# First tile of a pooled-attention and feed-forward kernel: batch 1's k and v pooled by vector engines instead of by matmuls, attention sums split from values, and the down matmuls over four accumulators

## The chip, the cores and the metric

The kernel runs on one core of one Trainium2 chip. A core has a matrix engine (TensorE, PE in the profile; its weight loads are shown apart as PEld), three engines for elementwise work (VectorE or DVE, ScalarE or ACT, GpSimd or POOL), a queue engine (SyncE, SP), and 16 DMA engines that move data between HBM and the on-chip memory. TensorE writes to PSUM, which has eight banks of 512 float32 per partition. Each engine works through its own instructions in order and waits for others by semaphores.

The metric is the time of one execution on the device, in microseconds (us).

## The reference

There are 8 batches of 8 heads with 576 rows of 64 elements, in q, k and v. The values that feed the second half are computed so:

```python
pool = 8                                  # Sp = 576 / 8 = 72 pooled rows
k_p = k.reshape(B, H, Sp, pool, D).mean(axis=3)
v_p = v.reshape(B, H, Sp, pool, D).mean(axis=3)
scores = scale * np.matmul(q, k_p.transpose(0, 1, 3, 2))
attn = softmax(scores)
x = np.matmul(attn, v_p)                  # then [4608 tokens, 512]
h = x @ w_in                              # 512 x 2048
g = h * np.cos(h)
out = g @ w_out                           # 2048 x 512, float32
```

The kernel computes in bfloat16 with float32 sums. It leaves the maximum out of the softmax, and it takes 1/sum as exp(-ln(sum)).

## The kernel before

**Tiles.** The 4608 tokens are worked in nine tiles of 512. A tile has an *up half* (`up_mm`, line 321): eight groups `fp` of 2 x 4 matmuls of 128x128 by 128x512, each group into one of three PSUM pairs `banks[0..2]` (two banks each); ScalarE takes the cosine (line 328), VectorE multiplies into `g_sb` (line 331). Then a *down half* (`down_mm`, line 334): 64 matmuls `(ms, fc)`, 16 for each of four blocks of 128 tokens, accumulated in the two single banks `obanks`; `down_out` copies a finished block out (line 340) and SP stores it (line 344).

**Attention.** Batch b's attention is worked while tile b-1 is (tile 0 for batch 1), by calls that are put between the down matmuls; batch 0's is worked at the start. One *unit* is 256 tokens of four heads; the batch has four units and a last segment `REST` of 64 tokens of all heads, which is done in the next tile. A unit goes: `scores` (four matmuls, line 214, into a PSUM pair, then Exp on ScalarE, line 221), then `values`: four matmuls (line 244) whose weights hold the pooled v of a head beside 64 columns of 8.0 (`vz`), so that the same matmul gives the weighted values and the softmax sum on different partitions; then Ln and Exp on ScalarE (lines 250, 251) and a multiply on VectorE (line 255) into `xT`, the up matmuls' input.

At the start, batch 0 uses a second form: `sums_first` (line 269), matmuls with weights of ones that give the sums alone, and `values_then` (line 283), matmuls with 64-wide weights that give the values alone, four each for a unit.

**Pooling.** There are two ways in the kernel. Batches 0 and 1 are pooled by TensorE: k and v are loaded in a layout of 128 partitions (`load_even`, `kv_even_tiles`), and matmuls with a 0/1 matrix `groups` add eight rows (`pool_k_mm`, line 160, 72 matmuls for a batch, whose results are copied into `kk` by line 132; `pool_v_mm`, line 168, 18 matmuls, copied into `vz` by line 170). From batch 2 on, k and v are loaded with the 72 pooled rows on partitions and eight rows behind each other (`load_kv`), and GpSimd adds halves three times (`pool_add`, lines 142, 145, 148 and 151); k's result `kp2` is then transposed by a DMA (`k_transpose`). Batch 0 and 1's q is transposed by TensorE in 18 matmuls with an identity (`q_transpose_mm`, line 195).

**Order.** The schedule is written by hand: each engine runs its instructions in the order of the code. In the down half of a tile, `fill` is a list of pairs (number of the down matmul before which it is put, call). In tile 0, the down matmuls go over two blocks `ms` at a time and, inside, over the four slices of `w_out`:

```python
mms = [(ms, fc) for hm in range(2) for cg in range(4) for ms in range(2 * hm, 2 * hm + 2)
       for fc in range(4 * cg, 4 * cg + 4)]
```

**Loads.** All loads but one are issued by POOL in the order of the code: q, k, v of batch 0; three of four slices of `w_in`; k of batch 1; half of its q; the last slice of `w_in`; the other half of q; `w_out` 0; v of batch 1; `w_out` 1 to 3; then, in tile 0, k, q and v of batch 2, whose adds stand behind them in POOL's order. `kv_st` has two buffers: batch 1's k and v lie in one, and batch 2's k and v take the two in turn.

The constants `dist` and `sign` are used at the start to make `groups`, and not later.

Of the kernel before, what the change touches and what calls it, by code (L numbers as in the profile page):

```python
# [9 lines left out]
FP32 = mybir.dt.float32  # L10
# [9 lines left out]
def kernel(  # L20
# [62 lines left out]
    def load_even(dst, b, src, j0=0, j1=KCH):  # L83
        nc.gpsimd.dma_start(out=dst[:, j0:j1].rearrange("p j t d -> p j (t d)"), in_=even_view(src, b, j0, j1))

    def kv_tile():
        return kvst.tile([128, 2 * H * POOL * D], BF16, name="kv_st", tag="kv_st")
# [9 lines left out]
    def q_tile(b):  # L97
        staged["q", b] = qst.tile([128, KCH, ROW, D], BF16, name="q_b", tag="q_b")

    def load_kv(b, which, src):  # L100

        st = kv_tile()[:Sp].rearrange("p (i h t d) -> p i h t d", i=2, h=H, t=POOL)
        nc.gpsimd.dma_start(out=st[:, 0].rearrange("p h t d -> p h (t d)"),
                            in_=src[b].rearrange("h (p t) d -> p h (t d)", t=POOL))
        staged[which, b] = st

    def load_q(b):
        q_tile(b)
# [2 lines left out]
    def load_w_in(cg):  # L111
        nc.gpsimd.dma_start(
            out=w_in_sb[cg],
            in_=moe_w_in[:, cg * 512:(cg + 1) * 512].rearrange("(k p) f -> p k f", p=128))

    def load_w_out(cg):
        nc.gpsimd.dma_start(
            out=w_out_sb[cg],
            in_=moe_w_out[cg * 512:(cg + 1) * 512, :].rearrange("(f p) m -> p f m", p=128))
# [5 lines left out]
    def v_part(b):  # L125
        return vz[b % 2][:, :, 0:4:3, :]
# [4 lines left out]
            for r in range(2):  # L131
                copy(out=dst[half[r], pj0:pj1, a, 0:Sp], in_=ps[half[a]])

    def pool_add(b, which, part=None):

        st = staged[which, b]
        x = st[:, 0]
        s = st[:, 1].rearrange("p h t d -> p (h t d)").bitcast(FP32).rearrange(
            "p (h t d) -> p h t d", h=H, t=POOL // 2)
        add = nc.gpsimd.tensor_tensor  # L140
        if part != 1:
            add(out=s, in0=x[:, :, 0:4, :], in1=x[:, :, 4:8, :], op=ADD)  # L142
        if part == 0:
            return
        add(out=s[:, :, 0:2, :], in0=s[:, :, 0:2, :], in1=s[:, :, 2:4, :], op=ADD)  # L145
        if which == "k":
            for slot in range(2):
                add(out=kp2[b % 2][:Sp, :, slot, :], in0=s[:, :, 0, :], in1=s[:, :, 1, :], op=ADD)  # L148
        else:
            s = s.rearrange("p (j a) t d -> p j a t d", a=2)  # L150
            add(out=v_part(b), in0=s[..., 0, :], in1=s[..., 1, :], op=ADD)

    def pool_k_mm(b, bank, pj0, pj1):

        kb = staged["k", b]
        ps = bank[:, 0:(pj1 - pj0) * Sp].rearrange("p (j n) -> p j n", n=Sp)
        for pj in range(pj0, pj1):
            for t in range(ROW):
                for rows in half:
                    nc.tensor.matmul(ps[rows, pj - pj0, :], lhsT=kb[rows, pj, t, :], rhs=groups[rows, t, :],  # L160
                                     start=(t == 0), stop=(t == ROW - 1))
        return lambda copy: put_kk(b, ps, pj0, pj1, copy)
# [10 lines left out]
    def k_transpose(b):  # L173
        nc.sync.dma_start_transpose(out=kk[b % 2], in_=kp2[b % 2].rearrange("p h s d -> p (h s d)"))


    QB = KCH * ROW // 2

# [84 lines left out]
    def sums_first(b, u, cs):  # L263

        (c0, n), (h0, nh) = u
        ex = att["ex", b, u]
        for i in range(nh):
            hp = i % 2
            nc.tensor.matmul(cs[hp * 64:hp * 64 + 64, (i // 2) * n:(i // 2 + 1) * n], lhsT=ones[:Sp, :],
                             rhs=ex[:, ex_col(u, i):ex_col(u, i) + n])  # L270
# [4 lines left out]
        att["inv", b, u] = inv  # L275

    def values_then(b, u, ao):

# [103 lines left out]
    dist = consts.tile([128, ROW, Sp], FP32, name="dist")  # L382
    sign = consts.tile([128, ROW, Sp], FP32, name="sign")
# [10 lines left out]
    half_pi = consts.tile([128, 1], FP32, name="half_pi")  # L394
    nc.vector.memset(half_pi, math.pi / 2.0)

    kv_even_tiles(1)
    q_tile(1)
    for cg in range(3):
        load_w_in(cg)  # L400
    load_even(staged["k", 1], 1, k)
    load_even(staged["q", 1], 1, q, 0, 2)
    load_w_in(3)
    load_even(staged["q", 1], 1, q, 2, 4)
    load_w_out(0)
    load_even(staged["v", 1], 1, v)
    nc.gpsimd.memset(vz[1], float(POOL))
    for i in range(2):
        nc.gpsimd.memset(kp2[i], 0.0)
    for cg in range(1, 4):  # L410
        load_w_out(cg)

    def warm_up(n, bank):

# [41 lines left out]
    for t in range(NT):  # L456
        b = t + 1
        if t > 0:

            up_mm(t, 0, 0, 2)  # L460
            up_mm(t, 1, 0, 2)
        for fp in range(FFCH // 2):
            up_mm(t, fp, 2 if fp < 2 else 0)
            between = ()
            if t == 0:
                if fp == 4:
                    puts = pool_k_mm(1, obanks[0], 0, 2), pool_k_mm(1, obanks[1], 2, 4)
                elif fp in (5, 6):
                    g0 = 9 * (fp - 5)
                    puts = q_transpose_mm(1, obanks[0], g0, g0 + 5), q_transpose_mm(1, obanks[1], g0 + 5, g0 + 9)  # L470
                if fp in (4, 5, 6):
                    puts[0](vec)
                    between = ((puts[1], act),)
            up_g(t, fp, between)
            if 0 < t and b < B:
                if fp == 0:
                    q_transpose(b)
                elif fp == 2:
                    k_transpose(b)
                    if t == 1:  # L480
                        load_next(b)
                        pool_add(b, "v", 1)
                        load_kv(b + 1, "v", v)
        mms = [(ms, fc) for ms in range(4) for fc in range(FFCH)]
        if t == 0:
            mms = [(ms, fc) for hm in range(2) for cg in range(4) for ms in range(2 * hm, 2 * hm + 2)
                   for fc in range(4 * cg, 4 * cg + 4)]


        def S_(n, bank):  # L490
            return lambda: scores(b, us[n], banks[bank])

        later = []

        def V_(n, bank, wait=None):
            return lambda: values(b, us[n], banks[bank], wait)

        fill = []
        if t < B:
            exp_tables()  # L500
            fill = [(1, lambda: scores(t, REST, banks[2])), (16, lambda: values(t, REST, banks[1]))]
        if t == 0:
            fill[1:] = [(2, S_(0, 0)), (8, lambda: pool_v_mm(1, banks[1])), (8, lambda: values(t, REST, banks[2])),
                        (11, S_(1, 0)), (13, V_(0, 1)), (18, S_(2, 2)), (21, V_(1, 0, later)), (26, S_(3, 1)),
                        (32, lambda: later.pop()()), (32, V_(2, 2)), (40, V_(3, 0))]
        elif b < B:
            us = BY_TOKENS

            def scores_of(*parts):

                def go():
                    for f in scores_mm, scores_exp:
                        for b_, u, bank in parts:
                            f(b_, u, banks[bank])
                return go

            def rows_of(i, blk, bank):
                return lambda: values_rows(b, us[2 * i:2 * i + 2], blk, banks[bank])

            fill = [(4, scores_of((b, us[0], 2), (b, us[1], 0))), (18, rows_of(0, 0, 1)), (19, rows_of(0, 1, 2)),  # L520
                    (29, scores_of((b, us[2], 0), (b, us[3], 1), (t, REST, 2))),
                    (42, rows_of(1, 0, 0)), (44, rows_of(1, 1, 1)), (47, lambda: values(t, REST, banks[2]))]
        fi = 0
        if t == NT - 1:
            mms = mms[:-FFCH]
        for n, (ms, fc) in enumerate(mms):
            while fi < len(fill) and fill[fi][0] <= n:
                fill[fi][1]()
                fi += 1
            down_mm(obanks[ms % 2], ms, fc)  # L530
            if fc == FFCH - 1:
                down_out(t, ms, obanks[ms % 2])
        if t < B:
            sin_tables()
        if b + 1 < B:
            if t != 1:
                load_next(b)
                load_kv(b + 1, "v", v)
            pool_add(b + 1, "k")
            pool_add(b + 1, "v", 0 if t == 0 else None)  # L540
# [29 lines left out]
```

## Time and profile before

| what | value |
|---|---|
| time, median of 3 runs | 296.92 us (296.73 to 298.92) |
| the profiled execution: its time and its span | 296.36 us, 294.6 us |
| mean granted TensorE clock | 0.998 of full |
| PE, DVE, ACT, POOL busy | 98%, 54%, 55%, 44% of the span |
| DMA queue that POOL issues to | 18.07 MB, 39.4% of the 16 engines' time |
| up matmuls (line 321) | 576, 126.6 us busy |
| down matmuls (line 334) | 560, 131.4 us busy |
| score matmuls (line 214) | 192, 11.9 us busy |
| GpSimd's first pooling add (line 142) | 12, mean 4058 ns |
| tile 0's up half | 17.21 to 33.59 us |
| tile 0's down half | 33.59 to 52.96 us |
| tile 1 | 52.96 to 83.32 us |

A row of a timeline has the start, the length, the engine, the line in the code, the operation, output <- input, the shape and the count; in square brackets stands the idle time of the engine before it and what ended that. The chain of work that ended last is followed back from the last instruction: at each step to what released it. All times are microseconds from the start of the span. Matmuls are pipelined, so the time of one in a chain is the distance to the next, and its own row is longer.

### The profile page before, as it was taken

To read this page: it belongs to the slowest core of one execution; us is meant where nothing else is said; L and a number is where in the kernel's file an instruction comes from. 1 tells how busy PE (TensorE), PEld (TensorE's weight loads), DVE (VectorE), ACT (ScalarE), POOL (GpSimd) and SP (SyncE) were. 2 spreads that over 40 slices of the span, in tenths; PEclk is the share of its full clock that TensorE was granted. 3 is DMA by queue.
4 is the path that set the end of the run, shared out by engine and by line. 5 is a ranking of instruction groups with operands and counts; after the bars stand their busy time and mean duration, and the time that the engine had idled before them with its cause. 6 is when DMAs were issued, how large, how long until landed. Compare 5 with 4: busy or idle time off the path is not lost.

```text
span 294.6 us, 4775 instructions
## 1 busy us (share of the span) xinstructions
PE 287.7 (98%) x1912; PEld 140.2 (48%) x1912; DVE 158.8 (54%) x212; ACT 162.1 (55%) x182; POOL 130.5 (44%) x93
## 2 busy tenths in 40 slices
PE   8899999999999999999999999999999999999995
PEld 3545544444544454445444544455445544444444
DVE  5458647466347643764375456645574557416612
ACT  3886898365446734673468337743675456506500
POOL 8563017968973696349833983399000000000000
PEclk9999999999999999999999999999999999999999
DMA  7999999659966975698469747994603320131033
GB/s 151 204 207 206 207 205 207 137 95 178 157 155 93 167 128 131 112 170 149 108 122 169 147 92 139 162 148 103 142 2 71 81 64 0 36 73 36 0 71 73
DMA packets 57222, 36.07 MB, mean 122 GB/s; under 512 B 35185, under 2 KB 52465, under 8 KB 57201
## 3 DMA queue, kind: packets, MB, share of 16 engines
q0 software_dynamic: 19744, 18.07, 39.4%
q1 hardware_dynamic: 37216, 17.57, 28.6%
q8 instruction: 15, 0.25, 0.4%
q10 hardware_dynamic: 240, 0.13, 0.2%
q14 instruction: 7, 0.05, 0.0%
HBM read 36.70 MB, written 9.44 MB: 157 GB/s over the span
## 4 chain that ended last, share of the span: by engine, by line
PE 93%; DVE 1%; issue 0%; DVEq 0%
PE bank L321 42%; PE obank L334 42%; PE bank L214 3%; PE bank L301 2%; PE bank L244 1%; PE bank L352 1%; PE obank L160 0%; PE bank L168 0%; PE obank L283 0%; PE obank L195 0%; DVE xT L285 0%; DVE vz L170 0%; DVE o_sb L340 0%; DVEq L285 0%
## 5 line engine op out<-in xcount | busy, mean ns | idle before, releaser
L334 PE MATMUL obank<-w_out_sb,g_sb 128*128 128x512 bf16 x560 | 131.4, 379 | 0.0
L321 PE MATMUL bank<-xT,w_in_sb 128*128 128x512 bf16 x576 | 126.6, 379 | 0.0
L328 ACT ACTIVATE cos<-bank,half_pi 128x1024 f32<-128x1024 f32 x72 | 79.3, 1114 | 70.4 <-PE bank L321 70.4
L331 DVE TENSOR_TENSOR g_sb<-bank,cos 128x1024 bf16<-128x1024 f32 x72 | 87.3, 1223 | 51.6 <-ACT cos L328 51.6
L321 PEld LDWEIGHTS <-w_in_sb 128*128 128x128 bf16 x576 | 56.1, 98 | 67.6 <-issue 1.6
L334 PEld LDWEIGHTS <-g_sb 128*128 128x128 bf16 x560 | 51.6, 98 | 56.6 <-issue 2.0
L142 POOL TENSOR_TENSOR kv_st<-kv_st 72x2048 f32<-72x2048 bf16 x12 | 48.7, 4058 | 30.4 <-DMA kv_st<-in_k_dram 30.4
L340 DVE COPY o_sb<-obank 128x512 f32<-128x512 f32 x35 | 24.2, 692 | 46.9 <-PE obank L334 46.7
L221 ACT ACTIVATE ex<-bank 72x1024 bf16<-72x1024 f32 (+1 forms) x40 | 35.0, 929 | 21.2 <-PE bank L214 21.1
L145 POOL TENSOR_TENSOR kv_st<-kv_st 72x1024 f32<-72x1024 f32 x12 | 28.2, 2348 | 0.9
L250 ACT ACTIVATE lnc<-bank 64x256 f32<-64x256 f32 (+1 forms) x24 | 10.8, 449 | 17.9 <-PE bank L244 17.7
L255 DVE TENSOR_TENSOR xT<-bank,inv 64x256 bf16<-64x256 f32 (+1 forms) x24 | 12.3, 511 | 10.8 <-ACT inv L251 10.6
L304 DVE TENSOR_TENSOR x_r<-bank,inv_r 128x512 bf16<-128x512 f32 x24 | 16.6, 691 | 0.8
L148 POOL TENSOR_TENSOR kp<-kv_st 72x512 bf16<-72x512 f32 x12 | 14.9, 1265 | 0.5
L214 PE MATMUL bank<-qT,kk 64*72 64x256 bf16 (+1 forms) x192 | 11.9, 250 | 0.4 <-DVE qT L196 0.4
L214 PEld LDWEIGHTS <-kk 64*72 64x72 bf16 x192 | 7.9, 110 | 8.7 <-issue 7.4
L309 ACT ACT_TABLE_LOAD x9 | 11.5, 1283 | 0.9 <-PEq L554 0.7
L312 ACT ACT_TABLE_LOAD x9 | 11.5, 1283 | 0.2
L301 PEld LDWEIGHTS <-ex 72*128 72x128 bf16 x192 | 8.9, 97 | 5.0
L452 POOL COPY gate<-kk 1x1 bf16<-1x1 bf16 x5 | 0.9, 180 | 22.7 <-DMA kk<-kp 22.7
L302 DVE RECIPROCAL inv_r<-bank 128x8 f32<-128x8 f32 x24 | 4.8, 202 | 10.7 <-PE bank L301 10.7
L301 PE MATMUL bank<-vz,ex 72*128 72x65 bf16 x192 | 9.8, 192 | 0.0
(59 smaller groups left out, 113.9 us busy)
## 6 DMA issues: line engine op xcount, KB each, us to landing
out_dram<-o_sb SPq DMA_DIRECT2D x70, 128.0 KB, 2.4
kv_st<-in_v_dram POOLq DMA_DIRECT2D x8, 576.0 KB, 12.9
kv_st<-in_k_dram POOLq DMA_DIRECT2D x7, 576.0 KB, 7.9
q_b<-in_q_dram POOLq DMA_DIRECT2D x6, 576.0 KB, 10.0
w_in_sb<-in_moe_w_in_dram POOLq DMA_DIRECT2D x4, 512.0 KB, 13.4
w_out_sb<-in_moe_w_out_dram POOLq DMA_DIRECT2D x4, 512.0 KB, 18.2
q_b<-in_q_dram POOLq DMA_DIRECT2D x4, 288.0 KB, 12.2
g_sb<-in_k_dram SPq DMA_DIRECT2D x1, 576.0 KB, 3.6
```

Of the source, the lines that this page charges most:

```text
L142: add(out=s, in0=x[:, :, 0:4, :], in1=x[:, :, 4:8, :], op=ADD)
L145: add(out=s[:, :, 0:2, :], in0=s[:, :, 0:2, :], in1=s[:, :, 2:4, :], op=ADD)
L148: add(out=kp2[b % 2][:Sp, :, slot, :], in0=s[:, :, 0, :], in1=s[:, :, 1, :], op=ADD)
L214: nc.tensor.matmul(pair[:Sp, bank, c:c + n].rearrange("p (g n) -> p g n", n=64), lhsT=kk[b % 2][half[r], h0 + i, 0:Sp], rhs=att["qT", b][h ...
L221: nc.scalar.activation(out=ex[:, 0:nh * n].rearrange("p (a n) -> p a n", a=2), in_=pair[:Sp, :, 0:nh * n // 2], func=ACTF.Exp, scale=scale ...
L301: nc.tensor.matmul(out[:, pj, hp * (D + 1):(hp + 1) * (D + 1)], lhsT=ex[:, c:c + 128], rhs=v1)
L304: nc.vector.tensor_mul(out=x, in0=vals, in1=inv.unsqueeze(3).to_broadcast([128, KCH, 2, D]))
L321: nc.tensor.matmul(h[:, j, :], lhsT=w_in_sb[fc // 4][:, ki, (fc % 4) * 128:(fc % 4 + 1) * 128], rhs=xT[:, ki, t * TILE:(t + 1) * TILE], st ...
L328: nc.scalar.activation(out=cos, in_=h, func=ACTF.Sin, bias=half_pi[:, :1])
L331: nc.vector.tensor_mul(out=g_sb[:, 2 * fp:2 * fp + 2, :], in0=h, in1=cos)
L334: nc.tensor.matmul(o, lhsT=g_sb[:, fc, ms * 128:(ms + 1) * 128], rhs=w_out_sb[fc // 4][:, fc % 4, :], start=(fc == 0), stop=(fc == FFCH - 1))
L340: nc.vector.tensor_copy(out=o[:, 0:n], in_=ps)
```

## The change

It has five parts, all around tile 0.

1. Batch 1's k and v are loaded as those of later batches are, with 72 pooled rows on partitions, each in two halves of four heads, and are pooled by `pool_add`: k by GpSimd, v by VectorE, in halves of four heads. k's result is transposed by TensorE (`k_transpose_mm`, new: four matmuls with an identity for four heads, one copy), and not by a DMA. The 72 + 18 pooling matmuls of batch 1 are gone.
2. The order of POOL's loads and instructions before tile 0 is other: see the diff. Two of the buffers for constants, `dist` and `sign`, now lie in the memory of `w_out` 2 and 3.
3. In tile 0 the scores of batch 1 go two units at a time, and `sums_two` and `values_two` (new) take the place of `values`: first the sums of two units by matmuls with ones, with one Ln and one Exp for both; later the values of the two with one multiply.
4. The second half of q's transposes moves from the up half (group 6) to down matmul 14; the first half moves from group 5 to 6. The last segment of batch 0 moves from down matmuls 1 (scores) and 8 (values) to 44 and 52.
5. Tile 0's down matmuls go over the slices of `w_out` outermost, with all four blocks open in four accumulators: the two banks of `banks[2]` and the two `obanks`. The four blocks end with matmuls 51, 55, 59 and 63; the first is copied out with the second.

```diff
-    def load_kv(b, which, src):
+    def load_kv(b, which, src, h0=0, h1=H):
...
+        if (which, b) not in staged:
+            staged[which, b] = kv_tile()[:Sp].rearrange("p (i h t d) -> p i h t d", i=2, h=H, t=POOL)
+        nc.gpsimd.dma_start(out=staged[which, b][:, 0, h0:h1].rearrange("p h t d -> p h (t d)"),
+                            in_=src[b, h0:h1].rearrange("h (p t) d -> p h (t d)", t=POOL))
...
-    def pool_add(b, which, part=None):
+    def pool_add(b, which, part=None, add=nc.gpsimd.tensor_tensor, h0=0, h1=H):
...
+    def k_transpose_mm(b, bank, h0, h1):
+
+        ps = bank.bitcast(BF16)[:, 0:(h1 - h0) * Sp].rearrange("p (h n) -> p h n", n=Sp)
+        for h in range(h0, h1):
+            nc.tensor.matmul(ps[:, h - h0, :], kp2[b % 2][:Sp, h].rearrange("p s d -> p (s d)"), identity[:Sp, :Sp],
+                             is_transpose=True)
+        nc.vector.tensor_copy(out=kk[b % 2][:, h0:h1, 0:Sp], in_=ps)
...
+    def sums_two(b, us_, pair):
+
+        for u, cs in zip(us_, (pair[:, 0, :], pair[:, 1, :])):
+            (c0, n), (h0, nh) = u
+            for i in range(nh):
+                hp = i % 2
+                nc.tensor.matmul(cs[hp * 64:hp * 64 + 64, (i // 2) * n:(i // 2 + 1) * n], lhsT=ones[:Sp, :],
+                                 rhs=att["ex", b, u][:, ex_col(u, i):ex_col(u, i) + n])
+        inv = asb.tile([128, 2, 512], FP32, name="inv2", tag="inv2", bufs=2)
+        nc.scalar.activation(out=inv, in_=pair, func=ACTF.Ln)
+        nc.scalar.activation(out=inv, in_=inv, func=ACTF.Exp, scale=-1.0)
+        att["inv", b, us_] = inv
+
+    def values_two(b, us_, pair):
+
+        for i, u in enumerate(us_):
+            (c0, n), (h0, nh) = u
+            ex = att.pop(("ex", b, u))
+            for k in range(nh):
+                pj, hp = divmod(h0 + k, 2)
+                nc.tensor.matmul(pair[hp * 64:hp * 64 + 64, i, (k // 2) * n:(k // 2 + 1) * n],
+                                 lhsT=vz[b % 2][:, pj, 3 * hp, :], rhs=ex[:, ex_col(u, k):ex_col(u, k) + n])
...
+        nc.vector.tensor_mul(out=x, in0=pair.rearrange(both, n=n),
+                             in1=att.pop(("inv", b, us_)).rearrange(both, n=n))
...
-    kv_even_tiles(1)
     q_tile(1)
     for cg in range(3):
         load_w_in(cg)
-    load_even(staged["k", 1], 1, k)
+    load_kv(1, "k", k, 0, 4)
+    load_w_in(3)
     load_even(staged["q", 1], 1, q, 0, 2)
-    load_w_in(3)
+    load_w_out(0)
+    load_kv(1, "k", k, 4, 8)
     load_even(staged["q", 1], 1, q, 2, 4)
-    load_w_out(0)
-    load_even(staged["v", 1], 1, v)
-    nc.gpsimd.memset(vz[1], float(POOL))
     for i in range(2):
         nc.gpsimd.memset(kp2[i], 0.0)
-    for cg in range(1, 4):
-        load_w_out(cg)
+    nc.gpsimd.memset(vz[1], float(POOL))
+    load_w_out(1)
+    load_kv(1, "v", v, 0, 4)
+    pool_add(1, "k", h0=0, h1=4)
+    load_w_out(2)
+    load_kv(1, "v", v, 4, 8)
+    load_w_out(3)
+    pool_add(1, "k", h0=4, h1=8)
...
             if t == 0:
-                if fp == 4:
-                    puts = pool_k_mm(1, obanks[0], 0, 2), pool_k_mm(1, obanks[1], 2, 4)
-                elif fp in (5, 6):
-                    g0 = 9 * (fp - 5)
-                    puts = q_transpose_mm(1, obanks[0], g0, g0 + 5), q_transpose_mm(1, obanks[1], g0 + 5, g0 + 9)
-                if fp in (4, 5, 6):
+                if fp == 6:
+                    puts = q_transpose_mm(1, obanks[0], 0, 5), q_transpose_mm(1, obanks[1], 5, 9)
                     puts[0](vec)
                     between = ((puts[1], act),)
+                elif fp == 7:
+                    k_transpose_mm(1, obanks[0], 0, 4)
...
         if t == 0:
-            mms = [(ms, fc) for hm in range(2) for cg in range(4) for ms in range(2 * hm, 2 * hm + 2)
-                   for fc in range(4 * cg, 4 * cg + 4)]
+            mms = [(ms, fc) for cg in range(4) for ms in range(4) for fc in range(4 * cg, 4 * cg + 4)]
...
+        def late_q():
+            puts = q_transpose_mm(1, banks[0][:, 0, :], 9, 14), q_transpose_mm(1, banks[0][:, 1, :], 14, 18)
+            for put in puts:
+                put(vec)
+
+        def pool_v(h0):
+            return lambda: pool_add(1, "v", add=nc.vector.tensor_tensor, h0=h0, h1=h0 + 4)
+
+        early, late = tuple(us[0:2]), tuple(us[2:4])
+
+        def sums_values():
+            sums_two(1, late, banks[0])
+            values_two(1, early, banks[1])
...
         if t == 0:
-            fill[1:] = [(2, S_(0, 0)), (8, lambda: pool_v_mm(1, banks[1])), (8, lambda: values(t, REST, banks[2])),
-                        (11, S_(1, 0)), (13, V_(0, 1)), (18, S_(2, 2)), (21, V_(1, 0, later)), (26, S_(3, 1)),
-                        (32, lambda: later.pop()()), (32, V_(2, 2)), (40, V_(3, 0))]
+            fill = [(10, scores_of((1, us[0], 0), (1, us[1], 1))), (14, late_q), (18, lambda: sums_two(1, early, banks[1])),
+                    (22, lambda: k_transpose_mm(1, banks[0][:, 0, :], 4, 8)), (23, pool_v(0)),
+                    (27, scores_of((1, us[2], 0), (1, us[3], 1))), (35, sums_values), (36, pool_v(4)),
+                    (44, lambda: scores(0, REST, banks[1])), (52, lambda: values_two(1, late, banks[0])),
+                    (52, lambda: values(0, REST, banks[1]))]
...
+        acc = [obanks[ms % 2] for ms in range(4)]
+        if t == 0:
+            acc = [banks[2][:, 0, :], banks[2][:, 1, :], obanks[0], obanks[1]]
...
-            down_mm(obanks[ms % 2], ms, fc)
-            if fc == FFCH - 1:
-                down_out(t, ms, obanks[ms % 2])
+            down_mm(acc[ms], ms, fc)
+            if fc == FFCH - 1 and (t > 0 or ms > 0):
+                for m in range(0 if t == 0 and ms == 1 else ms, ms + 1):
+                    down_out(t, m, acc[m])
```

More of the change, by code (lines that the diff above doesn't have):

```diff
@@ L98, in q_tile @@
         staged["q", b] = qst.tile([128, KCH, ROW, D], BF16, name="q_b", tag="q_b")
-    def load_kv(b, which, src):
[L102 to L105, printed above, removed]
+    def load_kv(b, which, src, h0=0, h1=H):
[3 more added lines that the diff above has]
+                            in_=src[b, h0:h1].rearrange("h (p t) d -> p h (t d)", t=POOL))
     def load_q(b):
@@ L132, in put_kk @@
                 copy(out=dst[half[r], pj0:pj1, a, 0:Sp], in_=ps[half[a]])
-    def pool_add(b, which, part=None):
+    def pool_add(b, which, part=None, add=nc.gpsimd.tensor_tensor, h0=0, h1=H):
         st = staged[which, b]
-        x = st[:, 0]
+        x = st[:, 0, h0:h1]
         s = st[:, 1].rearrange("p h t d -> p (h t d)").bitcast(FP32).rearrange(
-            "p (h t d) -> p h t d", h=H, t=POOL // 2)
-        add = nc.gpsimd.tensor_tensor
+            "p (h t d) -> p h t d", h=H, t=POOL // 2)[:, h0:h1]
         if part != 1:
@@ L147, in pool_add @@
             for slot in range(2):
-                add(out=kp2[b % 2][:Sp, :, slot, :], in0=s[:, :, 0, :], in1=s[:, :, 1, :], op=ADD)
+                add(out=kp2[b % 2][:Sp, h0:h1, slot, :], in0=s[:, :, 0, :], in1=s[:, :, 1, :], op=ADD)
         else:
             s = s.rearrange("p (j a) t d -> p j a t d", a=2)
-            add(out=v_part(b), in0=s[..., 0, :], in1=s[..., 1, :], op=ADD)
+            add(out=v_part(b)[:, h0 // 2:h1 // 2], in0=s[..., 0, :], in1=s[..., 1, :], op=ADD)
     def pool_k_mm(b, bank, pj0, pj1):
@@ L275, in sums_first @@
         att["inv", b, u] = inv
+    def sums_two(b, us_, pair):
[17 more added lines that the diff above has]
+                                 lhsT=vz[b % 2][:, pj, 3 * hp, :], rhs=ex[:, ex_col(u, k):ex_col(u, k) + n])
+        (c0, n), (h0, nh) = us_[0]
+        x = xT[:, h0 // 2:(h0 + nh) // 2, b * S + c0:b * S + c0 + 2 * n].rearrange("p j (i n) -> p i j n", i=2)
+        both = "p i (j n) -> p i j n"
+        nc.vector.tensor_mul(out=x, in0=pair.rearrange(both, n=n),
+                             in1=att.pop(("inv", b, us_)).rearrange(both, n=n))
     def values_then(b, u, ao):
@@ L381 @@
     make_identity(nc, identity)
-    dist = consts.tile([128, ROW, Sp], FP32, name="dist")
-    sign = consts.tile([128, ROW, Sp], FP32, name="sign")
+    dist, sign = (w.rearrange("p f m -> p (f m)").bitcast(FP32)[:, 0:ROW * Sp].rearrange("p (t n) -> p t n", n=Sp)
+                  for w in w_out_sb[2:4])
     groups = consts.tile([128, ROW, Sp], BF16, name="groups")
@@ L485, with scores_of, go @@
         if t == 0:
-            mms = [(ms, fc) for hm in range(2) for cg in range(4) for ms in range(2 * hm, 2 * hm + 2)
-                   for fc in range(4 * cg, 4 * cg + 4)]
[L490 to L496, printed above, removed]
+            mms = [(ms, fc) for cg in range(4) for ms in range(4) for fc in range(4 * cg, 4 * cg + 4)]
+        def scores_of(*parts):
+            def go():
+                for f in scores_mm, scores_exp:
+                    for b_, u, bank in parts:
+                        f(b_, u, banks[bank])
+            return go
+        def late_q():
[8 more added lines that the diff above has]
+            values_two(1, early, banks[1])
         fill = []
@@ L502 @@
         if t == 0:
-            fill[1:] = [(2, S_(0, 0)), (8, lambda: pool_v_mm(1, banks[1])), (8, lambda: values(t, REST, banks[2])),
-                        (11, S_(1, 0)), (13, V_(0, 1)), (18, S_(2, 2)), (21, V_(1, 0, later)), (26, S_(3, 1)),
-                        (32, lambda: later.pop()()), (32, V_(2, 2)), (40, V_(3, 0))]
+            fill = [(10, scores_of((1, us[0], 0), (1, us[1], 1))), (14, late_q), (18, lambda: sums_two(1, early, banks[1])),
[3 more added lines that the diff above has]
+                    (52, lambda: values(0, REST, banks[1]))]
         elif b < B:
             us = BY_TOKENS
[L509 to L515, printed above, removed]
             def rows_of(i, blk, bank):
```

## The prediction

> **What bounds the kernel.** I read the engines' shares first, then the chain that ended last, then that chain in order of time around tile 0, the only tile that the change touches.
>
> ```profile
> PE 287.7 (98%) x1912; PEld 140.2 (48%) x1912; DVE 158.8 (54%) x212; ACT 162.1 (55%) x182; POOL 130.5 (44%) x93
> ...
> PE 93%; DVE 1%; issue 0%; DVEq 0%
> ```
>
> TensorE (PE) is busy 98% of the span and is 93% of the chain, so time is won only by taking work off PE, and lost only where PE waits. The list of PE's waits has nothing between 17 and 52 us. The same chain in order of time (start, length, what):
>
> ```profile
> 17.21 8.79 PE bank L321 x40
> 26.01 1.29 PE obank L160 x72
> 27.30 1.83 PE bank L321 x8
> 29.13 0.50 PE obank L195 x9
> ...
> 36.12 1.10 PE bank L168 x18
> 37.22 0.34 PE bank L244 x8
> ...
> 38.21 0.34 PE bank L214 x4
> 38.55 0.54 PE obank L334 x2
> 39.09 0.44 PE bank L244 x4
> ...
> 67.67 0.56 PE bank L214 x8
> 68.23 3.13 PE obank L334 x14
> ```
>
> Tile 0 runs from 17.21 to 52.96 us, where tile 1's first up matmul starts: 35.75 us. A full matmul costs 0.2164 us (64 of them stand in this chain as one piece of 13.85). Tile 0 has 64 up and 64 down ones, 27.70 us; the other **8.05 us are insertions** for batch 1, 2.53 in the up half (17.21 to 33.59) and 5.52 in the down half. A visit of score matmuls costs more than its own piece: the two down matmuls behind 38.21 take 0.54 and not 0.43, the 14 behind 67.67 take 3.13 and not 3.03, so 0.10 is added to each.
>
> **The change, part by part, on PE.**
>
> *Goes.* Pooling k by 72 matmuls: 1.29, and 0.10 on the eight behind it (1.83 for 1.73). Pooling v by 18 matmuls: 1.10. Four score visits of four: 4 x (0.34+0.10) = 1.76. Four values visits of four with 128-wide weights: 3 x 0.44, the last 0.61, together 1.93. Two q transposes of nine stay in number (0.50 each); the rest of the last segment stays (scores 0.26+0.10, values 0.34).
>
> *Comes.* Scores in two visits of eight: 2 x (0.56+0.10) = 1.32. Eight k transposes in two groups of four. Nine q transposes with 128 columns took 0.50, so four take 0.22; a visit may add 0.10, hence 0.25 to 0.35 a group. Sums and values of two units at a time, eight matmuls each with 64-wide weights. Their nearest rows are the start-up's:
>
> ```profile
> 15.32 0.41 PE L283 MATMUL obank<-ex,vz 72*64 72x256 bf16 x4 [0.28 <-DVE vz L170]
> 15.56 0.39 PE L283 MATMUL bank<-ex,vz 72*64 72x256 bf16 x4
> 15.78 0.38 PE L269 MATMUL bank<-ex,ones 72*64 72x256 bf16 x4
> ```
>
> From start to start four of them take 0.22 to 0.24, half of the 0.44 for four 128-wide ones. So splitting sums from values costs the same streaming: 0.44 for eight. A visit adds nothing (as line 244) up to 0.22 (as line 214: 0.56+0.10 against 0.44).
>
> Sum of what is inserted after: q 0.50+0.50; k 0.50 to 0.70; scores 1.32; sums of the first two units 0.44 to 0.66; sums of the last two with values of the first two 0.88 to 1.10; values of the last two 0.44 to 0.66; the rest segment's scores 0.36 and values 0.24 (tile 1's piece) to 0.34. That is 5.18 to 6.14, middle 5.66. **PE saves 8.05 - 5.66 = 2.4 us (1.9 to 2.9)** if it waits for nothing.
>
> The number of down matmuls does not change; they only go over four accumulators, for which the third bank pair is free since the up half's sixth group.
>
> The Trainium skill, "TensorE: Matmul & The Clock Gate", Part 4, speaks against the k transposes: it gives about 275 ns for a 128x128 transpose inside a kernel. By it eight would cost 2.2 us and the saving would be about 0.8 us; this trace has nine in 0.50 us, 56 ns each, and I take the trace.
>
> **What could be late.** With the middle costs PE's new times are: up half ends 31.56 (17.21+13.85+0.50), down starts 31.86; then the insertion before down matmul 10 falls at 34.0, 14 at 35.6, 18 at 36.9, 22 at 38.3, 27 at 39.7, 35 at 42.1, 44 at 45.1, 52 at 47.2; tile 1 starts at 50.6.
>
> POOL's rows give landings and adds:
>
> ```profile
> 21.20 0.74 POOL L117 DMA_DIRECT2D w_out_sb<-in_moe_w_out_dram  x1 [0.94 <-DMA w_in_sb<-in_moe_w_in_dram]
> 24.03 0.74 POOL L117 DMA_DIRECT2D w_out_sb<-in_moe_w_out_dram  x1 [2.08 <-DMA kv_st<-in_k_dram]
> ...
> 28.07 0.77 POOL L84 DMA_DIRECT2D q_b<-in_q_dram  x1 [1.41 <-DMA w_in_sb<-in_moe_w_in_dram]
> ...
> 46.28 4.06 POOL L142 TENSOR_TENSOR kv_st<-kv_st 72x2048 f32<-72x2048 bf16 x1 [7.92 <-DMA kv_st<-in_k_dram]
> 50.42 2.35 POOL L145 TENSOR_TENSOR kv_st<-kv_st 72x1024 f32<-72x1024 f32 x1
> 52.85 2.49 POOL L148 TENSOR_TENSOR kp<-kv_st 72x512 bf16<-72x512 f32 x2
> ```
>
> An issue that waits for a landing starts when it lands: the third w_in slice at 21.2, k of batch 1 at 24.0 (2.83 us for 576 KB, so a half load takes 1.4 us), w_in's last slice at 28.1, batch 2's k at 46.3. The transfers are the limit until then (DMA busy share above 1 in these windows), so I move landings by what stands ahead of them in the queue:
>
> - Half of k lands at 22.7; w_in's last slice moves ahead of half of k and half of q, to about 25.3. PE wants it at 27.6, since the shorter up half asks for it about 2 us sooner than before.
> - POOL issues w_out 1 and half of v first, past both waits, by 22.0, then adds half of k: (4.06+2.35+2.49)/2 = 4.5 us, done at 27.2. PE wants it at 31.6. Behind these adds stand the issues of w_out 2, half of v and w_out 3, now at 27 to 30 and not 21 to 25; five or more loads (over 1.8 MB, 9 us) are outstanding then, so the DMA engines don't run dry. The two extra issues (0.8 each) fall in the same idle time.
> - The other k half lands by 30.8, is pooled by 35.4, wanted at 38.3.
> - w_out 1 to 3: they had landed by 37.4, 40.0 and 42.6 before (their down matmuls ran then without waiting). They move by one load and a half, by a half, and by nothing: 34.5, 38.6, 42.6, wanted at 36.5, 41.5, 46.3.
> - v's halves land at about 36.5 and 40.5. Their adds are now VectorE's (DVE), which shows no such add in tile 0. The nearest row has two SBUF inputs of 648 elements in 0.83 us: 1.04 ns an element and 0.155. So 1024+512+256 elements are 2.3 us; from below, without a fixed part, 1.9; from above by POOL's own rows, 3.9. I take 2.3, the same engine. The first half runs at 38.8 to 41.1, used at 42.1. The second stands behind the first multiply (ready at 43.2, 1.22 by the g_sb row): 44.5 to 46.8, used at 47.2. Slack 0.4: at 3.9 us PE would wait 1.2. The last copies of the tile wait behind it on DVE but nobody needs them before 54.
> - Tile 1 needs the rest segment's values, which move from down matmul 8 to 52. In the trace they start at 37.16 and their multiply ends at 39.71, 2.55 us later; after, 47.7+2.55 = 50.3, wanted at 50.6. Slack 0.3.
> - Batch 2's v load waits for the second v half and no longer for the v matmuls: 46.9 instead of 37.5. POOL's adds of batch 2's k stand behind it: 47.7 instead of 46.3. They end at about 56.7 and their transpose lands near 60; tile 1's scores want it at 65 (67.6 before). The 8 output issues on SP all come at the tile's end, ahead of batch 2's q transpose, which has until 65 too.
>
> On ScalarE, Ln and Exp of two units at once replace two halves with shorter instructions (1.20+0.63 a unit before); none of it ends a wait.
>
> The Trainium skill, "SBUF — State Buffer", "Who interferes with whom", says that a VectorE instruction with two SBUF inputs and a GpSimd instruction that reads SBUF block each other for a whole instruction. No row of before shows such a pair. If they met, the wait would be up to 4 us; by the times above they don't meet, since POOL is through at 35.4 and its next add stands behind the v load that waits for DVE's last one.
>
> **The sum**: the profiled execution took 296.36 (span 294.6 and 1.8 around it). 296.36 - 2.4 = 294.0 with no wait; with 0.1 for small ones 294.1. The median shown, 296.92, is 0.56 above that execution; I name 294.3, between the two. A change of under 1% (3 us) can hardly be told from none in this kernel, and this one is worth 0.8%.
>
> **Rivals.**
> 1. *Slower: half of k is awaited whole.* If PE's first transposes wait for the last k add rather than for the first half's (place: end of the up half; one POOL chain writes both halves), PE stands from 31.6 to 35.4: 3.8 us, and everything behind follows. 296.4 - 2.4 + 3.8 = 297.8. It decides from the point where that add ends 2.4 us after 31.6. For it: POOL is in-order and has issues between the halves. Against: the first q transposes of batch 0 started at 7.33 when q's second half was still to land at 10.7, so parts of a tile are awaited apart. With w_out late on top, over 300.
> 2. *The gain goes into the two thin slacks.* DVE's v adds at the upper bound cost 1.2, and the late rest segment up to 0.7: 294.1 + 1.9 = 296.0, no change to speak of.
> 3. *All costs at their low ends*: 296.4 - 2.9 = 293.5, just beyond 1%.
> 4. *It doesn't do what it says*: the sums and values don't stream in pairs in mid-tile, 0.1 us a matmul and not 0.055: 32 of them, 1.5 us more, 295.6.
>
> **Chances.** The forecast's case (293.8 to 294.8) 0.55; rival 3 0.17; rivals 2 and 4 together 0.18; rival 1 and its kin 0.10. Range 293.2 to 296.8: it leaves out rival 1 and the edge of rival 3. Faster by over 1% means under 293.95, which takes rival 3 and the lower edge of the forecast: 0.32. Slower by over 1% means over 299.9, the worst of rival 1: 0.08. The rest, 0.60, is within 1%.
>
> **What the profile after would show.** Tile 1's first up matmul at 50.6 (right), 52 or later (rivals 2 and 4), 54 (rival 1). No L160 or L168 matmul between 17 and 53. POOL adds at 22.7 and near 31, DVE adds of about 1.2, 0.7 and 0.4 us. PE's waits in the tile empty; a wait on k's pooled tile is rival 1, one on vz or xT rival 2. Eight sums to the next matmul in 0.45 to 0.65 us; 0.9 is rival 4.

## The result and the profile after

The changed kernel takes 295.30 us (median of 10 runs, 294.41 to 295.78); the kernel before takes 296.63 (10 runs). The ratio is 0.9942, with a 95% interval of 0.9923 to 0.9962: 0.6% faster. The forecast was 294.3, 0.8%. The profiled execution took 294.91 us with a span of 292.8; the one before took 296.36 with 294.6.

The page's engine shares, and the line of the chain by engine:

```profile
PE 285.5 (98%) x1846; PEld 138.1 (47%) x1846; DVE 158.9 (54%) x210; ACT 157.6 (54%) x169; POOL 141.6 (48%) x103
...
PE 92%; DMA 5%; POOL 1%; DVE 1%; ACT 0%; issue 0%; POOLq 0%; DVEq 0%
```

PE is still 98% busy. New is a DMA in the chain: part of it is the start, where v of batch 0 is waited for as before, and part is at tile 2, below. The chain in order of time around tile 0 (start, length, what; in this kernel line 356 is the up matmul, 369 the down matmul, 202 the q and 180 the k transposes, 221 the scores, 290 and 304 the sums and values of two units, 251 the values of the last segment):

```profile
17.03 12.25 PE bank L356 x56
29.28 0.50 PE obank L202 x9
29.79 1.73 PE bank L356 x8
31.51 0.13 PE obank L180 x4
...
33.81 0.58 PE bank L221 x7
34.38 0.97 PE obank L369 x4
35.35 0.57 PE bank L202 x9
...
36.78 0.56 PE bank L290 x8
...
41.92 0.56 PE bank L290 x8
42.48 0.44 PE bank L304 x8
...
47.05 0.56 PE bank L304 x8
47.61 0.34 PE bank L251 x8
...
50.54 13.85 PE bank L356 x64
```

Tile 0 runs from 17.03 to 50.54: 33.51 us and not 35.75. With 128 matmuls at 0.2164 that leaves 5.81 us of insertions, where there were 8.05. There is no wait of PE in the tile. But the gain of 2.24 us does not all arrive at the end. The starts of the tiles:

| start of | before | after | earlier by |
|---|---|---|---|
| tile 0 | 17.21 | 17.03 | 0.18 |
| tile 1 | 52.96 | 50.54 | 2.42 |
| tile 2 | 83.32 | 81.34 | 1.98 |
| tile 3 | 113.67 | 111.87 | 1.80 |
| end of the span | 294.6 | 292.8 | 1.8 |

Between tile 1 and tile 3, 0.62 us are given back. The chain at the end of tile 1, first of the kernel before, then of the kernel after:

```profile
79.65 3.67 PE obank L334 x17
83.32 13.85 PE bank L321 x64
```

```profile
76.61 0.11 DVE inv_r L337
76.72 4.57 DMA xT<-x_r
81.29 0.05 issue
81.34 14.02 PE bank L356 x64
```

Before, PE goes from tile 1's last down matmuls into tile 2 without a step. After, tile 2 starts when a DMA transpose of x has landed, 4.57 us after its issue; the same transpose needed 2.5 us before. From tile 1's start to tile 2's a tile takes 30.36 us when nothing is waited for, so tile 2 was wanted at 80.90 and stands at 81.34, 0.44 later. The loss is a little larger than that. In the chain, a matmul that waited for nothing stands at the end of the row before it, about 0.17 us after its own row starts; one that waited stands at the start of its own row. Counted from row to row, tile 1 starts at 50.37 and tile 2 at 81.34, 30.97 us later. So the whole 0.62, within rounding, is lost at this one wait.

The steps that the prediction had put a time on, in VectorE's timeline of the kernel after (the first half of v):

```profile
38.71 1.21 DVE L141 TENSOR_TENSOR kv_st<-kv_st 72x1024 f32<-72x1024 bf16 x1
...
39.95 0.69 DVE L144 TENSOR_TENSOR kv_st<-kv_st 72x512 f32<-72x512 f32 x1
...
40.74 0.42 DVE L150 TENSOR_TENSOR vz<-kv_st 72x256 bf16<-72x256 f32 x1
```

2.32 us for half of v; 2.3 was forecast.

### The profile page after: what moved, and what is told of

It is laid out like the page before. It is cut to its first block, busy times and chain, and to the rows that moved or that the text cites. A ratio compares the mean times of both kernels' runs of the same rounds, so it can differ in the third digit from the quotient of the medians.

```text
span 292.8 us, 4637 instructions
## 1 busy us (share of the span) xinstructions
PE 285.5 (98%) x1846; PEld 138.1 (47%) x1846; DVE 158.9 (54%) x210; ACT 157.6 (54%) x169; POOL 141.6 (48%) x103
## 4 chain that ended last, share of the span: by engine, by line
PE 92%; DMA 5%; POOL 1%; DVE 1%; ACT 0%; issue 0%; POOLq 0%; DVEq 0%
PE bank L356 43%; PE obank L369 38%; DMA kv_st<-in_v_dram 3%; PE bank L221 3%; PE bank L369 2%; PE bank L336 2%; DMA xT<-x_r 2%; PE bank L387 1%; PE bank L251 1%; POOL q_b L84 1%; PE bank L290 0%; PE bank L167 0%; PE bank L304 0%; ACT ex L228 0%; DVE xT L320 0%
## 5 line engine op out<-in xcount | busy, mean ns | idle before, releaser
L369 PE MATMUL obank<-w_out_sb,g_sb 128*128 128x512 bf16 x528 | 123.9, 379 | 0.0
L141 POOL TENSOR_TENSOR kv_st<-kv_st 72x2048 f32<-72x2048 bf16 (+1 forms) x14 | 52.9, 3779 | 24.6 <-DMA kv_st<-in_k_dram 24.6
L375 DVE COPY o_sb<-obank 128x512 f32<-128x512 f32 x33 | 22.7, 691 | 44.4 <-PE obank L369 44.3
L144 POOL TENSOR_TENSOR kv_st<-kv_st 72x1024 f32<-72x1024 f32 (+1 forms) x14 | 30.7, 2194 | 1.0
L147 POOL TENSOR_TENSOR kp<-kv_st 72x512 bf16<-72x512 f32 (+1 forms) x16 | 17.8, 1129 | 0.6
L257 ACT ACTIVATE lnc<-bank 64x256 f32<-64x256 f32 x16 | 6.0, 378 | 19.2 <-PE bank L251 19.1
L104 POOL DMA_DIRECT2D kv_st<-in_v_dram x8 | 6.5, 818 | 10.4 <-DVE vz L150 8.7
L262 DVE TENSOR_TENSOR xT<-bank,inv 64x256 bf16<-64x256 f32 x16 | 6.8, 422 | 7.0 <-ACT inv L258 6.9
## 6 DMA issues: line engine op xcount, KB each, us to landing
kv_st<-in_v_dram POOLq DMA_DIRECT2D x7, 576.0 KB, 12.6
```

The lines of the kernel that those rows point to most:

```text
L147: add(out=kp2[b % 2][:Sp, h0:h1, slot, :], in0=s[:, :, 0, :], in1=s[:, :, 1, :], op=ADD)
L369: nc.tensor.matmul(o, lhsT=g_sb[:, fc, ms * 128:(ms + 1) * 128], rhs=w_out_sb[fc // 4][:, fc % 4, :], start=(fc == 0), stop=(fc == FFCH - 1))
L375: nc.vector.tensor_copy(out=o[:, 0:n], in_=ps)
```

## The experiments

My theory after the result: the work on PE fell as forecast, and the missing part is lost at tile 2 (about two thirds of it, as it turned out; the rest is told with the prediction below), because the last x transposes of tile 1 now meet batch 3's loads. Those loads hang on a chain of queues that tile 0's end sets in motion: SP issues tile 0's eight stores, then batch 2's q transpose, then its k transpose; POOL's gate waits for the k transpose before it loads batch 3. SP's rows, before and then after:

```profile
44.85 11.47 SPq L344 DMA_DIRECT2D out_dram<-o_sb  x8
56.52 2.16 SPq L187 DMA_TRANSPOSE qT<-q_b  x1
58.79 1.21 SPq L174 DMA_TRANSPOSE kk<-kp  x1
```

```profile
50.84 5.05 SPq L379 DMA_DIRECT2D out_dram<-o_sb  x8
56.07 3.47 SPq L194 DMA_TRANSPOSE qT<-q_b  x1
59.65 1.21 SPq L173 DMA_TRANSPOSE kk<-kp  x1
```

Before, the first stores went out from 44.85 on, while tile 0 was still at work. After, all eight come once the tile is over, one behind the other for 5.05 us, and the k transpose is issued 0.86 us later than before though PE is 2.4 us earlier. Counted from the end of tile 0 it is 3.3 us later: the last store goes 4.75 us behind that end and not 2.77, and the q transpose behind the stores holds SP for 3.47 us and not 2.16. Rivals: batch 2's v load, which now waits for VectorE (46.85 instead of 37.52) and has POOL's adds behind it, sets the loads; or the transposes are slow for another reason.

### The changed kernel once more

No edit.

> The changed kernel once more, as the measure for the runs beside it: 295.3 us, tile 1 from about 50.5 us and tile 2 about 0.4 us late, because the last x transposes of tile 1 by DMA land 4 us and more after their issue (4.57 in the first profile; 2.5 before the change).

295.21 us (6 runs), ratio 0.9951 (0.9932 to 0.9969). Tile 1 started at 50.46 and tile 2 at 82.29, 1.47 us late, the transpose landing 5.6 us after its issue. So the wait at tile 2 is there again, but its size is not fixed: 0.44 in one execution, 1.47 in the other (0.62 and 1.65 from row to row), whose times were 294.91 and 295.85.

### Batch 3's v load later

```diff
                         pool_add(b, "v", 1)
-                        load_kv(b + 1, "v", v)
...
             pool_add(b + 1, "k")
+            if t == 1:
+                load_kv(b + 1, "v", v)
             pool_add(b + 1, "v", 0 if t == 0 else None)
```

> The load of batch 3's v goes behind the adds of batch 3's k in POOL's order, so it is issued near 80 us instead of 68.7. Theory (loads and x transposes collide): with v's load out of the way, the x transposes that are issued near 76.7 land in about 2.5 us, tile 2's first up matmul starts near 80.9 without a wait, and the time falls by 0.6 us or more from 295.3, to about 294.4, with the runs closer together. Rival (the transposes are late for another reason, such as SP's queue or tile 1's own stores): the wait stays, 295.3.

301.88 us (4 runs), ratio 1.017 (1.0148 to 1.0193): slower by 6.7 us than the changed kernel. Where I had looked, the theory held: the x transpose issued at 76.83 landed in 2.4 us, and tile 2's first matmul came at 81.00, 30.35 after tile 1's. But the load had only been pushed on: it landed at 89.80, and behind the adds of v POOL came to batch 4's loads 8 us late, at 97.78 where the changed kernel has 89.80. There too the three go within 2.5 us, but here they go right ahead of tile 2's last x transposes. POOL's timeline, then the chain, of this kernel:

```profile
97.78 0.85 POOL L104 DMA_DIRECT2D kv_st<-in_k_dram  x1
98.63 0.78 POOL L84 DMA_DIRECT2D q_b<-in_q_dram  x1
99.40 0.84 POOL L104 DMA_DIRECT2D kv_st<-in_v_dram  x1
```

```profile
107.19 9.35 DMA xT<-x_r
116.53 0.14 issue
116.67 3.57 PE bank L356 x8
```

The transpose took 9.35 us, and PE waited 5.3 us for tile 3. Of the three loads k had landed at 106.39, before the transpose was issued; q landed at 110.9 and v, 15.7 us after its issue, at 115.12, and the transpose 1.4 us behind it. The cause is shown twice, then: no load in the way, 2.4 us; two loads in the way, 9.35. The wait is not the whole of the loss. The eight matmuls behind it took 3.57 us, where eight take 1.73: the granted TensorE clock was 0.50 from 116.6 to 120.3 us and 0.88 from there to 124.0, and the 22 matmuls up to 123.79 lost 2.4 us by it.

### Tile 0's stores behind batch 2's transposes

```diff
+    held = []
...
-            queues[i].dma_start(out=rows_of[b_, ORDER[pos], :, c0:c0 + n], in_=o[rows, 0:n])
+            dst, srcs = rows_of[b_, ORDER[pos], :, c0:c0 + n], o[rows, 0:n]
+            if t == 0:
+                held.append((dst, srcs))
+            else:
+                queues[i].dma_start(out=dst, in_=srcs)
...
                     k_transpose(b)
                     if t == 1:
+                        for dst, srcs in held:
+                            nc.sync.dma_start(out=dst, in_=srcs)
                         load_next(b)
```

> Tile 0's eight stores go behind the q and k transposes of batch 2 in SP's order. Theory (the stores, now all at the end of tile 0, hold up these transposes, and through POOL's gate on the k transpose the loads of batch 3): k's transpose is issued near 57 us instead of 59.65, batch 3's k load near 61 instead of 63.0, its v load near 66.7 instead of 68.7; it has landed by about 77.7, the x transposes meet less of it and tile 2 waits for 0.2 us or less: 294.7. Rival (the wait of batch 2's v load for VectorE sets POOL's order and the loads): batch 3's k load stays at 63, 295.3.

294.62 us (6 runs), ratio 0.9931 (0.9911 to 0.9952). SP's rows and POOL's load of batch 3's k:

```profile
49.95 5.59 SPq L195 DMA_TRANSPOSE qT<-q_b  x1
57.74 1.21 SPq L174 DMA_TRANSPOSE kk<-kp  x1
58.99 5.08 SPq L524 DMA_DIRECT2D out_dram<-o_sb  x8
```

```profile
61.81 0.87 POOL L105 DMA_DIRECT2D kv_st<-in_k_dram  x1
```

In this execution everything from tile 0 on was 0.9 us later (tile 0 from 17.94; the start-up had waited longer for its loads). Still k's transpose went out 1.9 us and batch 3's k load 1.2 us earlier than after. Tile 1 started at 51.44 and tile 2 at 81.79, 30.35 later: no wait. But one link of the theory did not hold. Batch 3's v load was issued at 67.47, 1.2 us earlier than after, and should have landed by about 77.7; it took 12.3 us instead of 11.0 and landed at 79.72, no sooner than after (79.67), and the transpose at 81.39. In this profile the wait is gone also because PE came 0.9 us later.

> Tile 0's stores behind the transposes of batch 2, once more: tile 2 starts 30.4 us after tile 1 without a wait, 294.6 us, 0.6 under the changed kernel. If the first result was chance, 295.2.

294.71 us (6 runs), ratio 0.9921 (0.9906 to 0.9936); tile 1 at 51.30, tile 2 at 81.77, 0.11 late. Here too tile 0 began late (17.80), and the load landed at 80.08. Both times the median is 0.5 to 0.7 us under those of the changed kernel (295.21 and 295.30), though the intervals of the ratios overlap. Against the kernel before, run beside each (296.47 and 296.89), the two are 1.85 and 2.18 us faster, the changed kernel 1.33 and 1.26. So the gain is seen in the medians; that it comes by an earlier landing of the load is not shown. This is the fastest version that was run.

The x transposes beside batch 3's v load, in the profiles where that load keeps its place ahead of them (us from the span's start; "wanted" is tile 1's start and 30.36):

| kernel | v load landed | transpose issued | landed | tile 2 wanted | tile 2 started |
|---|---|---|---|---|---|
| before | 76.9 | 79.15 | 81.62 | 83.32 | 83.32 |
| after | 79.7 | 76.72 | 81.29 | 80.90 | 81.34 |
| after, again | 80.6 | 76.65 | 82.25 | 80.82 | 82.29 |
| stores held | 79.7 | 77.63 | 81.39 | 81.80 | 81.79 |
| stores held, again | 80.1 | 77.49 | 81.72 | 81.66 | 81.77 |
| k by matmuls (below) | 82.7 | 78.56 | 84.11 | 82.73 | 84.16 |
| v by matmuls (below) | 82.8 | 79.58 | 84.29 | 83.75 | 84.33 |
| two blocks at a time (below) | 81.2 | 80.89 | 83.25 | 85.06 | 85.05 |
| adds on GpSimd (below) | 87.9 | 84.22 | 89.48 | 88.39 | 89.53 |

Where the load has two or more us to go at the transpose's issue, the transpose lands 1.4 to 1.7 us after the load, whenever it was issued. Where the load is through, or nearly, it takes 2.4 to 2.5. The table has the third of a tile's four x transposes, the one that PE waits for. In the seven profiles with two or more us to go the first of the four, issued about 6 us sooner, lands within 0.1 us of the load (79.64 and 79.67 in the changed kernel), the second 0.3 to 0.5 us later, and the third 1.1 to 1.3 us behind the second. (In the kernel before, the first landed 2.5 us after the load.) Whether the third waits for the load itself, or only for the two ahead of it that wait for the load, no run tells.

### Adds on GpSimd beside VectorE's

```diff
                 load_next(b)
+                if t == 0:
+                    for i in range(2):
+                        nc.gpsimd.tensor_tensor(out=xT[:Sp, 0, 2304:4352],
+                                                in0=w_in_sb[0][:Sp].rearrange("p k f -> p (k f)"),
+                                                in1=w_in_sb[1][:Sp].rearrange("p k f -> p (k f)"), op=ADD)
                 load_kv(b + 1, "v", v)
```

> Two adds of 72x2048 on GpSimd, each reading two inputs in SBUF, of which the results are not used, are put behind batch 2's q load: from about 38.2 to 46.4 us, beside VectorE's adds of v (38.7 to 41.2 and 44.2 to 46.6). If the two engines lock each other out, as the Trainium skill's page SBUF - State Buffer says, VectorE's 1.21 us add takes up to 4 us, values wait for vz and tile 1 starts 1 to 4 us later than 50.5. If they don't, all of VectorE's rows keep their length and the time is that of the changed kernel, 295.3.

303.08 us in one run (one profile, no interval). The timeline of this kernel:

```profile
37.54 9.08 POOL L588 TENSOR_TENSOR xT<-w_in_sb,w_in_sb 72x2048 bf16<-72x2048 bf16 x2
...
38.10 4.61 DVE L141 TENSOR_TENSOR kv_st<-kv_st 72x1024 f32<-72x1024 bf16 x1
...
42.75 4.43 DVE L144 TENSOR_TENSOR kv_st<-kv_st 72x512 f32<-72x512 f32 x1
...
47.28 0.42 DVE L150 TENSOR_TENSOR vz<-kv_st 72x256 bf16<-72x256 f32 x1
47.75 1.07 PE L304 MATMUL bank<-ex,vz 72*64 72x256 bf16 x8 [5.89 <-DVE vz L150]
```

VectorE's add of two SBUF inputs took 4.61 us instead of 1.21, the next 4.43 instead of 0.69. GpSimd's two adds, one row above, ran from 37.54 to 41.62 and from 41.70 to 46.62. The times fit turns of whole instructions, on both sides: VectorE's first add ended 1.09 us after GpSimd's first, about its own length; GpSimd's second add took 4.92 us, 0.84 more than its first; and VectorE's second ended 0.55 us after that. The third, with GpSimd idle, took its 0.42. PE waited 5.9 us, and the granted clock behind the wait was 0.50 (47.7 to 51.0 us) and 0.83 (to 54.0), so that tile 1 started at 58.03, 7.5 us later than in the changed kernel and not 1 to 4. So the rule of the Trainium skill, "SBUF — State Buffer", "Who interferes with whom", that two such instructions lock each other out, is seen here at full price, and in the changed kernel the two do not meet because GpSimd has nothing to do in that stretch: it stands at batch 2's v load, which waits for VectorE's last add of v. What looks like a loss in GpSimd's queue (8.67 us of waiting) keeps the two apart.

### Two blocks of down matmuls at a time

```diff
-            mms = [(ms, fc) for cg in range(4) for ms in range(4) for fc in range(4 * cg, 4 * cg + 4)]
+            mms = [(ms, fc) for hm in range(2) for cg in range(4) for ms in range(2 * hm, 2 * hm + 2)
+                   for fc in range(4 * cg, 4 * cg + 4)]
```

> The changed kernel with tile 0's down matmuls in the order of before (two blocks at a time, the slices of w_out inside). In the profile after, the slices 1 to 3 land at 35.4, 39.7 and 42.6 us; this order wants them before down matmuls 8, 16 and 24, near 33.4, 38.4 and 42.2 once the waits add up. Theory (the four accumulators are what lets batch 1's loads go ahead of w_out): PE waits 2.0, 1.3 and 0.4 us, tile 1 starts near 54, and the time is about 298 to 299 (up to 1 us may come back at tile 2, which then meets less of the loads). Rival (the order costs nothing): 295.2.

298.42 us (4 runs), ratio 1.0054 (1.0041 to 1.0067): slower than before. The chain of this kernel:

```profile
19.95 15.74 DMA w_out_sb<-in_moe_w_out_dram
35.69 0.04 issue
35.73 1.01 PE bank L369 x2
36.74 1.00 PE bank L221 x8
37.74 1.67 PE bank L369 x4
```

PE waited 2.1 us for w_out 1, which landed at 35.69, and for no load after that. But the three pieces behind the wait took 3.68 us, where the changed kernel has about 1.98 for the like (0.43, 0.58 and 0.97): the granted clock was 0.50 from 35.7 to 38.5 us, and 1.00 before. The waits of 1.3 and 0.4 that I had forecast did not come; the slow clock took as much, so that the time fell into the forecast by luck. Tile 1 started at 54.70. Tile 2 came 30.35 later, without a wait. In this order two blocks end in mid-tile, so that half of the stores go out from 46.19 on; the q transpose followed 2.9 us after tile 1's start (57.57) and batch 3's k load 10.4 (65.06), where the changed kernel has 5.5 and 12.5. That speaks for SP's stores as the cause at tile 2, as the run with the stores held does. The four accumulators are thus not a detail: the loads of batch 1 go ahead of w_out, and without the other order of down matmuls that alone loses more (3.9 us of tile 0, the slow clock included) than the rest wins.

### k or v by matmuls again

k: the loads become `load_even` of heads 0 to 3 and 4 to 7, the adds go, and

```diff
-                    k_transpose_mm(1, obanks[0], 0, 4)
+                    pool_k_mm(1, obanks[0], 0, 2)(vec)
...
-                    (22, lambda: k_transpose_mm(1, banks[0][:, 0, :], 4, 8)), (23, pool_v(0)),
+                    (19, lambda: pool_k_mm(1, banks[0][:, 0, :], 2, 4)(vec)), (23, pool_v(0)),
```

> The changed kernel with batch 1's k pooled by 72 matmuls again, in two groups of 36, and no adds and no transposes for it. By the rows of before, 1.29 and 0.10 behind it, less 0.27 for the eight transposes: tile 0 is 1.1 us longer than after, 296.3; since tile 2's wait for the x transposes may shrink as PE comes later, 295.5 at the least. If pooling k by matmuls had been hidden, 295.2.

297.89 us (9 runs), ratio 1.0048 (1.0019 to 1.0076): 2.6 to 2.7 above the changed kernel (2.3 if each is set against the kernel before run beside it, 296.89 and 296.47), about twice the forecast or more. Tile 0 took 34.96 us, 1.45 more than after, of which 1.40 and 0.10 behind are the 72 matmuls, less 0.26 for the eight transposes; about 0.2 is a wait of the first scores for k's copies. In this profile, 2.8 us longer than that of the changed kernel, 0.4 more is a later start of tile 0. The rest is again tile 2:

```profile
31.89 0.70 PE obank L159 x36
...
38.83 0.70 PE bank L159 x36
```

```profile
78.56 5.55 DMA xT<-x_r
```

The transpose landed at 84.11, and tile 2 was 1.43 late. The changed kernel's own two profiles have 0.44 and 1.47 there, so the edit need not have made this wait longer. I had expected that a later PE would wait less; but the stores and transposes of tile 0's end, and with them batch 3's loads, move along with PE (batch 3's k load 12.4 us after tile 1's start, after: 12.5).

v: the loads become `load_even`, and in the list `fill` (pieces of its lines)

```diff
-(23, pool_v(0)),
+(23, lambda: pool_v_mm(1, banks[1])),
...
- (36, pool_v(4)),
```

> The changed kernel with batch 1's v pooled by 18 matmuls again and not by VectorE: 1.10 us more on PE in tile 0, 296.3, less what tile 2's wait gives back, 295.5 at the least. Batch 2's v load then waits for PE (about 40) and not for VectorE (46.8), so GpSimd's adds of batch 2's k begin when k lands, near 46.4 and not 47.7. If that wait sets batch 3's loads, its k load comes near 61.7; if SP's stores ahead of the transposes do, it stays near 63.

298.07 us (11 runs), ratio 1.0050 (1.0031 to 1.0070). This does not give the price of v's matmuls alone: they need all of v at down matmul 23, and its second half landed only at 40.20, so PE waited 1.74 us for it beside the 1.17 of the matmuls (the chain of this kernel):

```profile
28.31 11.89 DMA kv_st<-in_v_dram
40.20 0.04 issue
40.24 1.17 PE bank L167 x18
```

It answers the other question. Batch 2's v load went at 41.72 and not 46.85, since it waited for PE and not for VectorE; yet batch 2's k transpose was issued at 62.48, right behind SP's stores (53.69 to 58.7) and the q transpose, while the adds of k, which began at 47.70 because k landed no sooner, had been done at 56.8. Batch 3's k load came at 66.0, 12.6 us after tile 1's start, as after (12.5). So SP's queue, the stores and the q transpose behind them, sets it, and not the v load.

## Why the prediction was right, and where it was not

- **What bounds the kernel** was read rightly: PE's work in tile 0, and nothing else in that tile. The forecast of tile 1's start was 50.6; it is 50.54. A little of that match is chance: tile 0 took 33.51 us where 33.4 was forecast, and began 0.18 earlier than before.
- **The sum of insertions** was 5.66 forecast and is 5.81. Eight sums, or eight values that stand alone, take 0.56 and 0.10 behind them, and values right behind sums 0.44 and 0.11: the upper end of what I had allowed. Four k transposes take 0.13, where I had 0.25 to 0.35. The Trainium skill, "TensorE: Matmul & The Clock Gate", Part 4, gives about 275 ns for one of 128x128 inside a kernel; in a row, those of 72x128 here come every 33 ns, and those of 128x128 every 56 to 63. The second nine q transposes take 0.57 and not 0.50. Sums and values stream two at a time: rival 4 is out. So is rival 3: 5.81 lies nearer the high end, 6.14, than the low one, 5.18.
- **What could be late** in tile 0 was sized well. Half of k landed at 22.87 (22.7 forecast), its adds ended at 27.8 (27.2), v's second half was ready at 46.55 and used at 46.98 (46.8 and 47.2). The slices of w_out came at 35.4, 39.7 and 42.6 (34.5, 38.6, 42.6): up to 1.1 later than forecast, still 1 us or more ahead of PE.
- **Rival 1** did not come: PE's first transposes began right after the up half, before GpSimd had pooled the other half of k (31.30 to 36.2). **Rival 2** is out for both of its places: no wait for vz, and tile 1 started as soon as PE was through with tile 0.
- **The step that failed** is the last under "What could be late", where I followed the eight stores and the later adds of batch 2 as far as tile 1's scores, "until 65", and stopped. Those were indeed in time. What hangs behind them is POOL's gate, then batch 3's loads, then the x transposes at tile 1's end, whose slack before was 1.7 us (landed 81.62, wanted 83.32), and PE had just been made 2.4 us earlier. That step had the k transpose landing near 60; behind the stores and the q transpose it landed at 62.39. The missed wait measured 0.62 in one profile and 1.65 in another.
- **A second term** was wrong without being noticed: "1.8 around it", the time of an execution outside the span, was carried over unchanged. In the runs with a span on record it is 1.7 to 1.9 for the kernel before and 2.1 to 2.2 for the changed one, without exception. Of the other versions only the one with v by matmuls has 1.7 to 1.8; so about 0.35 us comes with VectorE's pooling of v or its loads. No profile shows what lies there.
- **The account** of the profiled execution then closes to 0.03 us: 294.0 was forecast for it and it took 294.91. Tile 2's wait is 0.62 of the difference, the time outside the span 0.35, and the insertions 0.15, less the 0.18 by which tile 0 began sooner.
- The **time** of 294.3 was 1.0 too low, within the range of 293.2 to 296.8. Part of the distance to before was the choice of the base: ten runs of the kernel before have their median at 296.63, where three had it at 296.92, so that 294.3 would have been a fall of 2.3; it is 1.3. A change within 1% had been given the highest chance, 0.60, and it came.

What stays open: why the wait at tile 2 differs by 1 us between executions of one kernel. The start-up also varies (tile 0 began between 16.4 and 17.9 in these profiles), and no run tells the two apart. What v's matmuls alone would cost has not been measured without the wait for the load. The pairs of units, and the new places of q's second half and of the last segment, were not run apart from the rest; their prices are read from the chain.

## What to carry to other kernels

When PE is made faster in one stage, the slack of everything that comes later is smaller by that much: follow each queue that the change delays past its first reader, to the last transfer that still hangs on it. A transfer that PE waits for should not be issued behind bulk loads in flight; here DMA transposes landed with the load ahead of them or about 2 us behind it. And moving such a load later is no cure if it makes the loads behind it late in turn: that cost 6.7 us where the wait to be cured was about 1. When a wait is added up, look at the granted clock behind it too: what PE lost by it came on top of the wait.

## What was not expected

- A DMA transpose of x, the third of its tile, 2.4 to 2.5 us alone, took 3.8 to 5.6 us beside one load of 576 KB and 9.35 us behind two, landing 1.4 to 1.7 us after the last of them.
- Two VectorE adds of 1.21 and 0.69 us became 4.61 and 4.43 beside GpSimd adds of 4.08 and 4.92 us: a short instruction pays up to the whole length of the other engine's long one, and the next pays again.
- Behind waits of PE of 2.1, 5.3 and 5.9 us the granted clock was 0.50 for about 3 us; behind waits of 1.4, 1.5 and 1.7 us it stayed at 1.00. Where between 1.7 and 2.1 the change lies, no run tells.
- Transposes by TensorE of 72x128 take 33 ns each in a row of four, against 56 to 63 ns for 128x128 in rows of nine.
